# Attention with two mixture stages on one Trainium2 core: a hand order of three engines for the first eight head pairs

## The chip, the core and the metric

The kernel runs on one core of a Trainium2 chip. The core has TensorE (PE, with its weight loads as PEld), VectorE (DVE), ScalarE (ACT), GpSimd (POOL) and SyncE (SP), which only issues transfers here. GpSimd and ScalarE can issue transfers too. The metric is the device time of one launch in microseconds (us); lower is better.

## What is computed

Three stages follow each other: capped attention for 4 batches of 12 heads, 448 tokens, head size 64; a dense layer with a normalisation behind it; and a routed layer of eight experts, one for each token.

```python
scores = cap * tanh(q @ k.T / sqrt(D) / cap);  attn = exp(scores) / (sum + 1e-9);  x = attn @ v
h = x @ w_in;  solu = h * softmax(h);  ln = (solu - mean) / sqrt(var + 1e-6) * g_ln;  x = ln @ w_out
logits = x @ w_gate + modality_bias[modality_id];  e = argmax(logits);  gate = softmax(logits)[e]
out = gate * (relu(x @ w1[e]) @ w2[e])          # 1792 tokens, DM 768, DF 1024
```

## The kernel before

Heads are taken in 24 pairs, six to a batch. A pair is worked on in two units (cp 0 and 1), each with two of its four key chunks of 112. For pairs 0 to 7 ("plain") the scores are plain fp32 matmuls (a_scp, L664); from pair 8 on operands are split into high and low parts (a_split, a_sc). ScalarE does Tanh and Exp on each score tile (L667, L669). The value matmuls of a chunk (a_av, L714) come one unit behind its Exp. The sums over keys come straight from the exponentials by matmuls with a one-hot column for pairs below DIRECT = 6 (L720); from pair 6 on VectorE first adds the chunks (a_esp, L679 to L682) and one group of matmuls serves two pairs (L726). ScalarE or VectorE copies a pair's values to X (L729).

Meanwhile the weights w_in and w_out, which come as 64-bit words, are converted in 28 half blocks: GpSimd's queue loads one (conv_load, L450, four raw tiles), VectorE makes 32-bit numbers of it in three instructions (f64_to_f32, L426 to L428). For w_in (conv_in) ScalarE then casts a high part (L463) and VectorE subtracts (L464). For w_out (conv_out) VectorE scales by g_t and subtracts (L478, L479), TensorE transposes the block (conv_tr, L486), ScalarE copies the transposes (L488), and TensorE multiplies them by w_gate into eight more columns of w_out (conv_og, L494 to L496). Two blocks are converted in each unit (CUS), first the twelve of w_in, then the sixteen of w_out. The cast of a w_in block is put off to the next unit (defer(0)); conv_tr of the block before and conv_og stand right behind conv_out.

From unit 13 on batch 0 is finished: a_sums (L744), a_recip (L755 to L757), a_fin2 (L762 to L768). Then its token tiles are pushed: m_split, m_h (L536 to L538), m_act, m_tr (transposes L568, copies lh L576, ll L577) and m_y (L586 to L588) are a list of steps, which fill() deals out between the attention steps; pace() divides their cost by 27 + LEFT points, 33 for batch 1. Behind the attention come the routing and the expert slots: kinds D, H, F and T hold 512, 128, 256 and 32 tokens, in the order D, H, D, F, H, with T beside the first and third. Each block of expert weights is loaded by SP, cast by ScalarE (L1054) and subtracted by VectorE (L1055), some of them ahead of use; QH says how many steps before its end a slot H stops casting ahead.

What sets the order: inside manual_schedule the named engines keep the program's order. Before, that is TensorE alone up to the routing; ScalarE, VectorE, GpSimd and SP are ordered by the planner, by its own costs. PSUM has three slots of two banks for scores, transposes, logits, h and y (atile), one for values and one for sums. A tile's slot is freed when its last reader is done.

```python
with tc.manual_schedule(engines={mybir.EngineType.PE}):
    a_load(*pairs[0]); a_split(*pairs[0]); v_load(*pairs[0]); a_load(*pairs[1])
    ...
    setup_tables(xp)
    for n, (b, p) in enumerate(pairs):
```

Of the kernel before, what the change touches and what calls it, by code (L numbers as in the profile page):

```python
# [22 lines left out]
P = 128  # L23
# [36 lines left out]
TRP = (4, 0, 0)  # L60
TRO = 1
FIN = (2, 3, 4, 5, 5)
LEFT = (6, 6, 4)
RHA = 1
BIN = 0
SMD = (0, 1, 3, 4, 8, 12, 13)
# [16 lines left out]
def attn_moe_kernel(ctx, tc, qt, kt, vv, cap, w_in, w_out, g_ln, ids, w_gate, mbias, w1, w2, out):  # L83
# [49 lines left out]

    def setup_tables(tp):
        flat = tp.tile([P, NP, S], F32, tag="X", name="tmp").rearrange("p a b -> p (a b)")
# [12 lines left out]
        dve.tensor_add(sel, tmp, tmp2)  # L148
# [5 lines left out]
        pool.iota(pi, pattern=[[0, 1]], base=0, channel_multiplier=1, allow_small_or_imprecise_dtypes=True)  # L154
        pi2 = tm[:, 13:14]
# [5 lines left out]
        it = tm[:, 32:60].bitcast(I32).rearrange("p (t w) -> p t w", w=2)  # L161
        sp.dma_start(out=it, in_=ids)
        mb = tm[:, 64:80].rearrange("p (t w) -> p t w", w=NE)
        sp.dma_start(out=mb, in_=mbias)
# [12 lines left out]
        zr = flat[0:1, 2 * NP * P + 256:2 * NP * P + 256 + YW]  # L177
        dve.memset(zr, 0.0)
        sp.dma_start(out=ysc[0:1, :], in_=zr)

# [248 lines left out]

    later = {0: [], 1: [], 2: []}  # L430

    def defer(pos, f):
        if pos < 0:
            f()
        else:
            later[pos].append(f)

    def deferred(pos):
        while later[pos]:
            later[pos].pop(0)()  # L440

    blocks = [(w_in, 512, k, h) for k in range(ND) for h in range(2)] + \
        [(w_out, DM // 2, c, h) for c in range(NF) for h in range(2)]
    wraw = []

    def conv_load():
        if len(wraw) < len(blocks):
# [3 lines left out]
                         .bitcast(I32).rearrange("p (f t) -> p f t", t=2))  # L451
            wraw.append(raw)

    def conv_in(k, hf):
        raw = wraw[2 * k + hf]
        t = mp.tile([P, 512], I32, tag="x3", name=f"ti{k}_{hf}", bufs=4)
# [4 lines left out]

        def rest():
            act.copy(h_, tf)  # L463
            dve.tensor_sub(l_, tf, h_)  # L464

        defer(BIN, rest)

    wT = {}

    def conv_out(c, hf):  # L470
        HW_ = DM // 2
        raw = wraw[2 * ND + 2 * c + hf]
        t = mp.tile([P, HW_], I32, tag="x3", name=f"to{c}_{hf}", bufs=4)
# [5 lines left out]
        dve.scalar_tensor_tensor(l_, tf, g_t[:, c:c + 1], h_, op0=ALU.mult, op1=ALU.subtract)  # L479
        wT[c, hf] = tf  # L480

    def conv_tr(c, hf):
        tf = wT[c, hf]
        pt = atile(f"pt{c}_{hf}")[:, 0, :]
        for i in range(3):
            pe.transpose(pt[:, i * P:(i + 1) * P], tf[:, i * P:(i + 1) * P], ident)  # L486
        tt = mp.tile([P, 3, P], F32, tag="x3", name=f"wT{c}_{hf}", bufs=4)
        act.copy(tt, pt[:, :3 * P].rearrange("p (a b) -> p a b", a=3))  # L488
        wT[c, hf] = tt

    def conv_og(c):
        po = atile(f"po{c}")[:, 0, :]
        for i in range(ND):
            pe.matmul(po[:, :NE], wT[c, i // 3][:, i % 3, :], wg_t[:, i, :], start=(i == 0), stop=(i == ND - 1))  # L494
        act.activation(wouh[c][:, DM:YW], po[:, :NE], AF.Copy, scale=g_t[:, c:c + 1])
        dve.scalar_tensor_tensor(woul[c][:, DM:YW], po[:, :NE], g_t[:, c:c + 1], wouh[c][:, DM:YW],  # L496
                                 op0=ALU.mult, op1=ALU.subtract)

# [154 lines left out]
    def e_new(nm):  # L653
        return ap_.tile([CK, 2, S], F32, tag="e", name=nm, bufs=5)

    def a_scp(b, p, cp):

# [8 lines left out]
        for e, t in zip(es, ps):  # L666
            act.activation(e, t[:CK, :, :S], AF.Tanh, scale=sc8[:CK])  # L667
        for c, e in zip(chunks, es):
            act.activation(e, e, AF.Exp, scale=cap_t[:CK])  # L669
# [101 lines left out]

    crate = [0]
    convs = [(1, lambda k=k, h=h: conv_in(k, h)) for k in range(ND) for h in range(2)]
    for i in range(2 * NF + 2):
        if i < 2 * NF:
            convs.append((1, lambda c=i // 2, h=i % 2: conv_out(c, h)))
        if 0 < i <= 2 * NF:
            convs.append((0, lambda c=(i - 1) // 2, h=(i - 1) % 2: conv_tr(c, h)))
        if i > 1 and i % 2 == 1:
            convs.append((0, lambda c=(i - 3) // 2: conv_og(c)))  # L780

# [55 lines left out]

    with tc.manual_schedule(engines={mybir.EngineType.PE}):
# [6 lines left out]
        setup_tables(xp)  # L845
        for n, (b, p) in enumerate(pairs):
            for cp in range(2):
                if plain(b, p):
                    a_scp(b, p, cp)
                else:  # L850
                    a_sc(b, p, 0, cp)
                if cp == 0 and n:
                    a_av(*pairs[n - 1], chunks=(2, 3) if plain(*pairs[n - 1]) else range(4))
                elif cp and plain(b, p):
                    a_av(b, p, chunks=(0, 1))
                deferred(0)
                fill(FW[0])
                if b > 0:
                    finish(b - 1, 4 * p + 2 * cp)
                a_esp(b, p, cp)  # L860
                if cp == 0 and n + 1 < len(pairs):
                    a_split(*pairs[n + 1], js=(0,))
                if not plain(b, p):
                    a_sc(b, p, 1, cp)
                fill(FW[1])
                if cp == 1 and n + 1 < len(pairs):
                    a_split(*pairs[n + 1], js=(1,))
                if cp == 1 and n + 2 < len(pairs):
                    a_load(*pairs[n + 2])
                if cp == 0 and n + 1 < len(pairs):  # L870
                    v_load(*pairs[n + 1])
                fill(FW[2])
                while convs and (not convs[0][0] or CUS[crate[0]] <= 2 * n + cp):
                    crate[0] += convs[0][0]
                    convs.pop(0)[1]()
                if b > 0:
                    finish(b - 1, 4 * p + 2 * cp + 1)
        a_av(B - 1, NP - 1)
# [552 lines left out]
```

## Time and profile before

| | us |
|---|---|
| median of three runs | 782.14 (778.53 to 783.64) |
| the profiled execution | 780.17 |
| its span, first to last instruction | 778.4 |
| TensorE busy in the span | 733.1 (94%) |
| VectorE, ScalarE, GpSimd busy | 452.9, 392.1, 209.5 |

Times within the trace count from the span's start. A row of a timeline has start, duration, engine, line, operation, output and inputs, and a count when like instructions in a row are merged; in brackets stands how long the engine was idle before it and what released it. An fp32 matmul of the first eight pairs shows as two records, so x8 is four matmuls. In the table of stretches, PEclk is the granted TensorE clock: 1.00 is 2.4 GHz, 0.50 is 1.2 GHz, and means between them are a mixture of the two.

### The profile page before, as it was taken

Reading aid. Unit: us, or ns where it says so; the run is one execution under the profiler, and the core shown is the slowest. Engines: PE = TensorE matmul, PEld = TensorE weight load, DVE = VectorE, ACT = ScalarE, POOL = GpSimd, SP = SyncE. Lnnn points to the kernel's source line nnn. Section 1 sums busy time; section 2 is a strip of 40 time slices with the busy share of each in tenths; the row PEclk is TensorE's granted clock in tenths of the full one; section 3 lists DMA queues with packets and bytes.
Section 4 is the critical chain, followed back from the end, with each engine's and each line's share of the span. In section 5 each row is a group of like instructions: output and inputs, shape, how many; then the busy total and the mean of one; then the engine's idle time right before and its main releaser. Section 6 shows DMA issues by size and latency. Waiting matters only on the chain.

```text
span 778.4 us, 11381 instructions
## 1 busy us (share of the span) xinstructions
PE 733.1 (94%) x4150; PEld 575.0 (74%) x4150; DVE 452.9 (58%) x833; ACT 392.1 (50%) x541; POOL 209.5 (27%) x285
## 2 busy tenths in 40 slices
PE   6889889999999999999999999899999999999993
PEld 2235556777587787577878899789879988799982
DVE  5978766667757666674455744856146172563630
ACT  5987755776655464646641214434145171553530
POOL 4222013435352333345341214441210211002010
PEclk9999989999999999999999999999999999999996
DMA  9856302223312321322001303467937369485520
GB/s 290 295 175 170 100 14 71 83 84 91 94 53 75 91 75 43 103 54 74 22 0 42 123 21 123 143 236 253 385 106 250 132 202 395 162 262 172 205 79 23
DMA packets 39060, 104.50 MB, mean 134 GB/s; under 512 B 6439, under 2 KB 16689, under 8 KB 38994
## 3 DMA queue, kind: packets, MB, share of 16 engines
q1 hardware_dynamic: 32466, 74.26, 29.6%
q0 software_dynamic: 6528, 29.42, 10.9%
q8 instruction: 34, 0.56, 0.3%
q14 instruction: 32, 0.26, 0.1%
HBM read 92.58 MB, written 11.27 MB: 133 GB/s over the span
## 4 chain that ended last, share of the span: by engine, by line
PE 79%; DVE 7%; issue 6%; ACT 3%; DMA 3%; POOL 1%; SPq 0%; POOLq 0%; ACTq 0%; DVEq 0%
PE av L714 7%; PE h L536 5%; PE h L538 5%; PE h L537 5%; PE y L586 5%; PE y L588 5%; PE y L587 5%; PE sc L689 3%; PE sc L690 3%; PE poD L1178 3%; PE poD L1180 3%; PE poD L1179 3%; PE phD L1109 3%; PE phD L1110 3%; PE phD L1111 3%
## 5 line engine op out<-in xcount | busy, mean ns | idle before, releaser
L692 ACT ACTIVATE e<-sc,sc 112x896 f32<-112x896 f32 x64 | 64.5, 1008 | 76.6 <-PE sc L690 74.4
L714 PE MATMUL av<-e,v 112*64 112x448 f32 x384 | 81.3, 556 | 4.3 <-ACT e L669 2.4
L586 PE MATMUL y<-wouh,lh 128*128 128x388 f32 x224 | 77.1, 344 | 2.3 <-ACT lh L576 1.8
L588 PE MATMUL y<-wouh,ll 128*128 128x388 f32 x224 | 76.3, 341 | 0.3 <-DVE ll L577 0.2
L587 PE MATMUL y<-woul,lh 128*128 128x388 f32 x224 | 76.0, 339 | 0.0
L536 PE MATMUL h<-winh,xh 128*128 128x512 f32 x168 | 68.8, 410 | 1.5 <-ACT xh L523 1.5
L693 ACT ACTIVATE e<-e,cap_t 112x896 f32<-112x896 f32 x64 | 66.9, 1045 | 1.4
L538 PE MATMUL h<-winh,xl 128*128 128x512 f32 x168 | 66.7, 397 | 0.2 <-DVE xl L524 0.2
L537 PE MATMUL h<-winl,xh 128*128 128x512 f32 x168 | 66.3, 395 | 0.0
L714 PEld LDWEIGHTS av<-e,v 112*64 112x64 f32 x384 | 24.6, 138 | 52.8 <-issue 38.7
L701 POOL TENSOR_TENSOR es<-es,e 112x448 f32<-112x448 f32 x32 | 40.9, 1278 | 36.4 <-DVE es L700 33.0
L648 POOL TENSOR_TENSOR kl<-kr,kh 128x448 fp32r<-128x448 f32 x22 | 28.5, 1296 | 75.2 <-DVE kh L645 52.8
L586 PEld LDWEIGHTS y<-wouh,lh 128*128 128x128 f32 x224 | 42.1, 188 | 8.5 <-issue 4.3
L689 PE MATMUL sc<-qs,kh 128*112 128x448 f32 x128 | 47.3, 369 | 0.0
L690 PE MATMUL sc<-qs,kl 128*112 128x448 f32 x128 | 46.9, 366 | 0.0
L1055 DVE TENSOR_TENSOR wl_H<-raw_H,wh_H 128x768 fp32r<-128x768 f32 (+1 forms) x28 | 29.2, 1070 | 29.4 <-ACT wh_H L1054 29.4
L1055 DVE TENSOR_TENSOR wl_D<-raw_D,wh_D 128x768 fp32r<-128x768 f32 (+1 forms) x28 | 29.9, 1071 | 23.5 <-ACT wh_D L1054 23.2
L1178 PE MATMUL poD<-wh_D,hhD 128*128 128x384 f32 x128 | 43.0, 336 | 0.0
L588 PEld LDWEIGHTS y<-wouh,ll 128*128 128x128 f32 x224 | 42.1, 188 | 1.1 <-DVE ll L577 1.0
L1180 PE MATMUL poD<-wh_D,hlD 128*128 128x384 f32 x128 | 42.8, 334 | 0.0
L1179 PE MATMUL poD<-wl_D,hhD 128*128 128x384 f32 x128 | 42.8, 334 | 0.0
L587 PEld LDWEIGHTS y<-woul,lh 128*128 128x128 f32 x224 | 42.1, 188 | 0.8
(382 smaller groups left out, 1769.5 us busy)
## 6 DMA issues: line engine op xcount, KB each, us to landing
kr<-in_kt_dram SPq DMA_DIRECT2D x64, 112.0 KB, 2.6
qr<-in_qt_dram SPq DMA_DIRECT2D x64, 112.0 KB, 2.6
rawc<-in_w_in_dram POOLq DMA_DIRECT2D x12, 512.0 KB, 5.1
rawc<-in_w_out_dram POOLq DMA_DIRECT2D x16, 384.0 KB, 4.4
raw_D<-in_w_dram SPq DMA_DIRECT2D x12, 512.0 KB, 3.7
wr_T<-in_w_dram SPq DMA_DIRECT2D x16, 384.0 KB, 4.3
raw_D<-in_w_dram SPq DMA_DIRECT2D x16, 384.0 KB, 4.7
wr_T<-in_w_dram SPq DMA_DIRECT2D x12, 512.0 KB
```

What stands on the lines that cost most here:

```text
L536: pe.matmul(o, s["xh"][d], winh[d][:, c], start=(d == 0), stop=False)
L537: pe.matmul(o, s["xh"][d], winl[d][:, c], start=False, stop=False)
L538: pe.matmul(o, s["xl"][d], winh[d][:, c], start=False, stop=(d == ND - 1))
L586: pe.matmul(o, s["lh"][f], wouh[f][:, c], start=(f == 0), stop=False)
L587: pe.matmul(o, s["lh"][f], woul[f][:, c], start=False, stop=False)
L588: pe.matmul(o, s["ll"][f], wouh[f][:, c], start=False, stop=(f == NF - 1))
L689: pe.matmul(ps[:CK, c, :S], kh[:, k0:k0 + CK], qs, start=True, stop=False)
L690: pe.matmul(ps[:CK, c, :S], kl[:, k0:k0 + CK], qs, start=False, stop=True)
L693: act.activation(e, e, AF.Exp, scale=cap_t[:CK])
L714: pe.matmul(o[64 * j:64 * j + 64, :S], v[:, c, 64 * j:64 * j + 64], et[b, p, j, c], start=(c == 0), stop=(c == 3))
L1178: pe.matmul(p, hh[:, f, o], wh[:, c], start=(f == 0), stop=False)
L1179: pe.matmul(p, hh[:, f, o], wl[:, c], start=False, stop=False)
```

## The change

Pairs 0 to 7 (FIXED = 8) are put in a hand order for TensorE, ScalarE and VectorE together, in a new function unit(); pairs 8 to 23 go through the same function with TensorE alone ordered by hand. In a unit, conv_out no longer calls for its transposes at once: they go to a list "pe" that the next unit works off behind its scores, and conv_og to the list of the unit after that. The cast of a w_in block goes to a list "cast", worked off between the Tanh pair and the Exp pair, and the subtractions to "sub", worked off behind the conversions. The blocks of w_out and w_in alternate. The transposed block is kept in one tile of the tag ys instead of two of x3. setup_tables is split: the second half, which waits for the ids and biases, is at unit 3. g_t and wg_t are loaded by ScalarE's queue at the very start instead of SP's behind other loads. DIRECT becomes 8: pairs 6 and 7 are summed directly. For plain pairs finish() comes ahead of the values. QH's second number goes from 4 to 6, the second of LEFT from 6 to 7, and TRL = 3 puts the transposes of tile 9 (t = 9) three steps earlier in the list.

```diff
-DIRECT = 6
+DIRECT = 8
+FIXED = 8
-QH = (6, 4)
+QH = (6, 6)
+TRL = 3
-LEFT = (6, 6, 4)
+LEFT = (6, 7, 4)
...
+    def setup_second(tmp, tmp2, tm, ci, pi, it, mb):
+        dve.tensor_add(sel, tmp, tmp2)
...
-        sp.dma_start(out=g_t, in_=g_ln)
-        sp.dma_start(out=wg_t, in_=w_gate)
...
+    def flush(kind):
+        fs, later[kind] = later[kind], []
+        for f in fs:
+            f()
...
+    blocks = []
+    for i in range(2 * NF):
+        blocks.append((w_out, DM // 2, *divmod(i, 2)))
+        if i < 2 * ND:
+            blocks.append((w_in, 512, *divmod(i, 2)))
...
-        def rest():
+        def cast():
             act.copy(h_, tf)
-            dve.tensor_sub(l_, tf, h_)
+            later["sub"].append(lambda: dve.tensor_sub(l_, tf, h_))
-        defer(BIN, rest)
+        later["cast"].append(cast)
...
         wT[c, hf] = tf
+        later["pe"].append(lambda: conv_tr(c, hf))
...
+        act.copy(wT[c][:, 3 * hf:3 * hf + 3, :], pt[:, :3 * P].rearrange("p (a b) -> p a b", a=3))
+        if hf:
+            later["pe"].append(lambda: conv_og(c))
...
+    def unit(n, cp):
+        (b, p), u = pairs[n], 2 * n + cp
+        if plain(b, p):
+            a_scp(b, p, cp)
+            flush("pe")
+            flush("cast")
+            a_exp(b, p, cp)
+            if b > 0:
+                finish(b - 1, 4 * p + 2 * cp)
+        else:
+            a_sc(b, p, 0, cp)
+            flush("pe")
+            flush("cast")
+        if cp == 0 and n:
+            a_av(*pairs[n - 1], chunks=(2, 3) if plain(*pairs[n - 1]) else range(4))
+        elif cp and plain(b, p):
+            a_av(b, p, chunks=(0, 1))
+        fill(FW[0])
+        if b > 0 and not plain(b, p):
+            finish(b - 1, 4 * p + 2 * cp)
+        while convs and CUS[crate[0]] <= u:
+            crate[0] += 1
+            convs.pop(0)()
+        flush("sub")
+        if u == 3:
+            setup_second(*tables)
+        a_esp(b, p, cp)
...
+    with tc.manual_schedule(engines={ET.PE, ET.Activation, ET.DVE}):
+        act.dma_start(out=g_t, in_=g_ln)
+        act.dma_start(out=wg_t, in_=w_gate)
         a_load(*pairs[0])
-        a_split(*pairs[0])
         v_load(*pairs[0])
         a_load(*pairs[1])
         for _ in range(4):
             conv_load()
+        tables = setup_first(flat)
+        for n in range(FIXED):
+            unit(n, 0)
+            unit(n, 1)
+    with tc.manual_schedule(engines={ET.PE}):
+        for n in range(FIXED, len(pairs)):
+            unit(n, 0)
+            unit(n, 1)
...
-        msteps.insert(len(msteps) - TRO, (W[1], lambda: m_tr(t)))
+        msteps.insert(len(msteps) - TRO - TRL, (W[1], lambda: m_tr(t)))
```

## Rows read from the trace of the kernel before

**Rows 1.** Stretches: start:end, length, each engine's busy time, granted clock, DMA share, GB/s.

```profile
core 0: us, PE busy (x) PEld busy (x) DVE busy (x) ACT busy (x) POOL busy (x), PEclk, DMA share, GB/s
7.70:26.00 18.30, 16.92 (x82) 5.58 (x84) 13.74 (x32) 15.49 (x20) 3.09 (x6) 1.00 1.04 357
...
7.70:113.10 105.40, 92.90 (x506) 41.53 (x506) 80.24 (x174) 82.28 (x113) 17.20 (x28) 0.94 0.58 179
...
113.10:778.00 664.90, 640.22 (x3646) 533.43 (x3644) 369.71 (x651) 308.37 (x427) 185.74 (x243) 0.99 0.38 127
```

**Rows 2.** Two of the three stretches in which the granted clock is lower.

```profile
52.00:58.00 6.00, 6.00 (x27) 1.66 (x27) 3.06 (x7) 4.79 (x6) 0.98 (x2) 0.72 0.46 134
...
96.00:106.00 10.00, 8.22 (x35) 5.13 (x35) 3.48 (x9) 4.05 (x8) 0.00 (x0) 0.66 0.01 2
```

**Rows 3.** TensorE's waits, 7.7 to 114 us: total us, times, longest.

```profile
PE pt L486 <- DVE to L428: 4.1, 2, 2.0
PE av L714 <- ACT e L669: 2.4, 2, 1.4
PE po L494 <- ACT wT L488: 2.4, 3, 1.0
...
PE sc L664 <- DVE X L764: 1.6, 2, 1.2
```

**Rows 4.** Timeline of TensorE: one unit with two blocks, at full clock.

```profile
64.22 0.88 PE L486 MATMUL pt<-ident,to 128*128 128x128 f32 x6
64.93 1.42 PE L494 MATMUL po<-wg_t,wT 128*128 128x8 f32 x12
66.28 1.76 PE L664 MATMUL sc<-qr,kr 64*112 64x448 f32 x8
67.97 1.72 PE L714 MATMUL av<-e,v 112*64 112x448 f32 x8
69.63 0.96 PE L720 MATMUL S<-e,zone 112*32 112x448 f32 x8
70.52 0.87 PE L486 MATMUL pt<-ident,to 128*128 128x128 f32 x6
```

**Rows 5.** Timeline of TensorE: first scores, the end of batch 0, first h.

```profile
7.78 5.54 PE L664 MATMUL sc<-qr,kr 64*112 64x448 f32 x16 [7.78 <-DMA qr<-in_qt_dram]
...
100.87 0.92 PE L755 MATMUL rt<-ident,rr 112*44 112x112 f32 x4
...
106.45 1.49 PE L762 MATMUL rb<-rh,sel 128*128 128x448 f32 x6
...
113.16 0.50 PE L536 MATMUL h<-winh,xh 128*128 128x512 f32 x1
```

**Rows 6.** Timeline of ScalarE: two Tanh and two Exp.

```profile
13.88 1.89 ACT L667 ACTIVATE e<-sc,sc 112x896 f32<-112x896 f32 x2
15.66 1.97 ACT L669 ACTIVATE e<-e,cap_t 112x896 f32<-112x896 f32 x2
```

**Rows 7.** Stretch 7 to 113.1 us, instructions on es alone (PE, PEld, DVE, POOL).

```profile
7.00:113.10 106.10, 0.00 (x0) 0.00 (x0) 5.35 (x9) 0.00 (x0) 0.94 0.58 180
```

**Rows 8.** Timeline of VectorE: two independent neighbours, then two in a chain.

```profile
41.42 0.56 DVE L427 SCALAR_TENSOR_TENSOR to<-rawc,to 128x384 int32<-128x384 int32 x1
41.89 0.36 DVE L426 TENSOR_SCALAR to<-rawc 128x384 int32<-128x384 int32 x1
...
47.01 0.56 DVE L427 SCALAR_TENSOR_TENSOR to<-rawc,to 128x384 int32<-128x384 int32 x1
47.60 0.56 DVE L428 SCALAR_TENSOR_TENSOR to<-rawc,to 128x384 int32<-128x384 int32 x1
```

**Rows 9.** TensorE's waits, 630 to 645 us.

```profile
PE phD L1109 <- ACT txT L1206: 1.9, 1, 1.9
```

**Rows 10.** TensorE's waits, 404 to 414 us.

```profile
PE y L586 <- ACT lh L576: 0.9, 1, 0.9
```

**Rows 11.** DMA issues of the page: count, KB each, median us to landing.

```profile
rawc<-in_w_in_dram POOLq DMA_DIRECT2D x12, 512.0 KB, 5.1
```

More of the change, by code (lines that the diff above doesn't have):

```diff
@@ L154, in setup_tables @@
         pool.iota(pi, pattern=[[0, 1]], base=0, channel_multiplier=1, allow_small_or_imprecise_dtypes=True)
+        it = tm[:, 32:60].bitcast(I32).rearrange("p (t w) -> p t w", w=2)
+        sp.dma_start(out=it, in_=ids)
+        mb = tm[:, 64:80].rearrange("p (t w) -> p t w", w=NE)
+        sp.dma_start(out=mb, in_=mbias)
+        zr = flat[0:1, 2 * NP * P + 256:2 * NP * P + 256 + YW]
+        dve.memset(zr, 0.0)
+        sp.dma_start(out=ysc[0:1, :], in_=zr)
+        return tmp, tmp2, tm, ci, pi, it, mb
+    def setup_second(tmp, tmp2, tm, ci, pi, it, mb):
+        dve.tensor_add(sel, tmp, tmp2)
         pi2 = tm[:, 13:14]
@@ L428, in f64_to_f32 @@
         dve.scalar_tensor_tensor(dst, lo, 29, dst, op0=ALU.logical_shift_right, op1=ALU.bitwise_or)
-    later = {0: [], 1: [], 2: []}
-    def defer(pos, f):
-        if pos < 0:
-            f()
[L435 to L444, printed above, removed]
+    later = {"pe": [], "cast": [], "sub": []}
+    def flush(kind):
+        fs, later[kind] = later[kind], []
+        for f in fs:
+            f()
+    blocks = []
[3 more added lines that the diff above has]
+            blocks.append((w_in, 512, *divmod(i, 2)))
+    wraw, rawof = [], {}
     def conv_load():
@@ L452, in conv_load @@
             wraw.append(raw)
+            rawof[src is w_in, k, h] = raw
     def conv_in(k, hf):
-        raw = wraw[2 * k + hf]
+        raw = rawof[True, k, hf]
         t = mp.tile([P, 512], I32, tag="x3", name=f"ti{k}_{hf}", bufs=4)
@@ L471, in conv_out @@
         HW_ = DM // 2
-        raw = wraw[2 * ND + 2 * c + hf]
+        raw = rawof[False, c, hf]
         t = mp.tile([P, HW_], I32, tag="x3", name=f"to{c}_{hf}", bufs=4)
@@ L486, in conv_tr @@
             pe.transpose(pt[:, i * P:(i + 1) * P], tf[:, i * P:(i + 1) * P], ident)
-        tt = mp.tile([P, 3, P], F32, tag="x3", name=f"wT{c}_{hf}", bufs=4)
-        act.copy(tt, pt[:, :3 * P].rearrange("p (a b) -> p a b", a=3))
-        wT[c, hf] = tt
+        if hf == 0:
+            wT[c] = mp.tile([P, YW], F32, tag="ys", name=f"wT{c}", bufs=1)[:, :DM].rearrange("p (a b) -> p a b", b=P)
+        act.copy(wT[c][:, 3 * hf:3 * hf + 3, :], pt[:, :3 * P].rearrange("p (a b) -> p a b", a=3))
+        if hf:
+            later["pe"].append(lambda: conv_og(c))
     def conv_og(c):
@@ L493, in conv_og @@
         for i in range(ND):
-            pe.matmul(po[:, :NE], wT[c, i // 3][:, i % 3, :], wg_t[:, i, :], start=(i == 0), stop=(i == ND - 1))
+            pe.matmul(po[:, :NE], wT[c][:, i, :], wg_t[:, i, :], start=(i == 0), stop=(i == ND - 1))
         act.activation(wouh[c][:, DM:YW], po[:, :NE], AF.Copy, scale=g_t[:, c:c + 1])
-        dve.scalar_tensor_tensor(woul[c][:, DM:YW], po[:, :NE], g_t[:, c:c + 1], wouh[c][:, DM:YW],
-                                 op0=ALU.mult, op1=ALU.subtract)
+        later["sub"].append(lambda: dve.scalar_tensor_tensor(
+            woul[c][:, DM:YW], po[:, :NE], g_t[:, c:c + 1], wouh[c][:, DM:YW], op0=ALU.mult, op1=ALU.subtract))
     rpool = []
@@ L667, in a_scp, with a_exp @@
             act.activation(e, t[:CK, :, :S], AF.Tanh, scale=sc8[:CK])
-        for c, e in zip(chunks, es):
+        exps[b, p, cp] = es
+    def a_exp(b, p, cp):
+        for c, e in zip((2 * cp, 2 * cp + 1), exps.pop((b, p, cp))):
             act.activation(e, e, AF.Exp, scale=cap_t[:CK])
@@ L772, in attn_moe_kernel @@
     crate = [0]
[L773 to L780, printed above, removed]
+    convs = [lambda f=conv_in if src is w_in else conv_out, k=k, h=h: f(k, h) for src, _, k, h in blocks]
     msteps, drained = [], set()
@@ L836, in finish @@
             pace(3 * (2 * NP - (FIN[4] + 1) // 2) + LEFT[b])
-    with tc.manual_schedule(engines={mybir.EngineType.PE}):
+    def unit(n, cp):
[25 more added lines that the diff above has]
+        a_esp(b, p, cp)
+        if cp == 0 and n + 1 < len(pairs):
+            a_split(*pairs[n + 1], js=(0,))
+        if not plain(b, p):
+            a_sc(b, p, 1, cp)
+        fill(FW[1])
+        if cp == 1 and n + 1 < len(pairs):
+            a_split(*pairs[n + 1], js=(1,))
+        if cp == 1 and n + 2 < len(pairs):
+            a_load(*pairs[n + 2])
+        if cp == 0 and n + 1 < len(pairs):
+            v_load(*pairs[n + 1])
+        fill(FW[2])
+        if b > 0:
+            finish(b - 1, 4 * p + 2 * cp + 1)
+    ET = mybir.EngineType
+    flat = xp.tile([P, NP, S], F32, tag="X", name="tmp").rearrange("p a b -> p (a b)")
+    with tc.manual_schedule(engines={ET.PE, ET.Activation, ET.DVE}):
+        act.dma_start(out=g_t, in_=g_ln)
+        act.dma_start(out=wg_t, in_=w_gate)
         a_load(*pairs[0])
-        a_split(*pairs[0])
         v_load(*pairs[0])
@@ L844, in attn_moe_kernel @@
             conv_load()
[L845 to L877, printed above, removed]
+        tables = setup_first(flat)
[6 more added lines that the diff above has]
+            unit(n, 1)
         a_av(B - 1, NP - 1)
```

13 lines of the change are left out of this document (2 added, 11 removed).

## The prediction

> **What bounds the kernel now.** The first view is the table of stretches, which splits the span where the first h matmul starts [rows 1]. Behind it TensorE is busy 640.2 of 664.9 us, and the next engine, VectorE, 370: that stage is TensorE's own work, and nothing that this change does to its work list matters there. Ahead of it, from the first score matmul at 7.78 to the first h matmul at 113.16 [rows 5], TensorE is busy 92.9 of 105.4 us and its clock averages 0.94, while VectorE (80.2) and ScalarE (82.3) are loaded but not full [rows 1]. So the first sixteen units (a unit is half a pair: four of its eight score matmuls) run at (113.2 - 7.8) / 16 = 6.6 us each, and some of that is waiting. The second view says what for: the 12.5 us of idle time are transposes waiting for a w_out block that VectorE has only just made (4.1), the logit matmuls waiting for ScalarE's copy of those transposes (2.4), the value matmuls waiting for Exp (2.4), scores waiting for X (1.6), and smaller ones [rows 3]. Both of the first two come from the code: conv_tr and conv_og stand directly behind conv_out in TensorE's hand order. The third view shows a second price: the granted clock falls to the 1.2 GHz level in three stretches, each some microseconds behind such a wait; two of them are shown, 6 us at a mean of 0.72 (the third is like it) and 10 us at 0.66, so 1.7 + 1.7 + 3.4 = 6.8 us are lost to half speed [rows 2].
>
> **The change, part by part.** *The order of the first eight pairs.* Transposes of a block now come one unit after its conversion, its logit matmuls one unit later still, behind the scores, and the cast of a w_in block between the Tanh pair and the Exp pair. What TensorE then has to do up to the first h is a sum of groups at full clock, start to start [rows 4]: 16 units of scores at 1.69 = 27.0; 15 of values at 1.66 = 24.9; 16 transposes of half a block at 0.71 / 2 = 5.7; 8 logit groups at 1.35 = 10.8; sums by direct matmul in 15 units at 0.89 = 13.4; the reciprocal and fin2 steps 0.9 + 1.5 [rows 5] and as much as the reciprocal again for a_sums (an estimate, 0.9). Together 85.1, from 7.8: 92.9 us. The direct sums of pairs 6 and 7 are in it with 3 x 0.89 = 2.7 that were not there before; the fourth group falls behind the first h, where one group of the old sums goes.
>
> To that come waits that I expect to stay. In the first units nothing hides Exp: by the sum of its groups TensorE could start unit 4 at about 24.7, while ScalarE, at 1.78 for two Tanh start to start and 1.97 for two Exp [rows 6], with the first copies and casts between, lets it at about 26.3: 1.6. Around fin2 the scores wait for X as now, 1.6 [rows 3], the reciprocal of batch 0 stands on VectorE behind the last two conversions, about 0.5, and the split behind the last Exp, about 0.6: 2.7 (the last two estimates). A logit tile keeps one of three PSUM slots until VectorE's subtraction, which now stands behind that unit's two conversions and, from unit 3 on, behind setup_second too. If the next scores take another slot, that costs nothing; if the planner gives them this one, up to 2.6, half of VectorE's 5.0 us a unit (worked out below), which is the most that I see it trail there. I take 1.3. Small waits that I cannot place: between 0 and the 12.5 of now; I take 2, nearer to 0 because the two largest causes are named and moved. The clock: between 0 and the 6.8 of now; I take 0, because each of the three falls follows waits of 0.6 to 2.0 us on the moved steps, and the stretch to 26 us, with 1.4 us of idle time in it, shows 1.00 [rows 1]. First h at 92.9 + 1.6 + 2.7 + 1.3 + 2 = 100.5 against 113.2: 12.7 us saved.
>
> *The other engines have to hold that pace.* ScalarE's work there does not change: 82.3 of what becomes 92.7 us, 89%. VectorE loses nine adds, 5.35, from this stretch [rows 7], but a block's conversion is now issued as an unbroken chain. Instructions that depend on each other start 0.59 apart where the same kind behind an independent one needs 0.47 [rows 8]: 0.12 a link, four links in each of 16 w_out blocks and two in each of 12 w_in blocks, 10.6 us if none was chained before, 0 if all were. Some of those chains were unbroken already (the second pair of [rows 8] is one), so I take half: 80.2 - 5.4 + 5.3 = 80.1 of 92.7, 86%, or 5.0 a unit. Covered, but the cover is thin, and that is a rival below.
>
> The Trainium skill (VectorE: DVE Perf Modes, The DRAIN you can't avoid) says that the next operation cannot issue before the pipe is empty, whether or not operations are chained by semaphores. By it the chain would cost nothing and VectorE would come to 74.9; the 0.59 against 0.47 of [rows 8] disagree, and the rows decide.
>
> *g_t and wg_t by ScalarE's queue.* w_out blocks come first now, so VectorE needs g_t for its very first block instead of behind twelve others. It is moved ahead of SP's q, k and v loads and past the small tables on that queue; two issues on ScalarE, which has no work before the first scores, cost nothing. Had it stayed on SP, it would have held VectorE until those loads were done. Splitting the setup takes the wait for the ids away from VectorE's head; at unit 3 it costs the VectorE time counted above. The transposed copy in the ys tile instead of x3 is one tile per block; its next writer stands behind the logit matmuls of the block before on TensorE, so no new wait.
>
> *Later edits.* TRL puts the transposes of tile 9 three steps, some 1.6 us, ahead: the 0.9 wait for lh goes [rows 10]. QH lets slot H cast fewer blocks ahead: before, ScalarE's copy txT stood behind casts that waited for their DMA, and TensorE waited 1.9 for it [rows 9]; now one such cast is ahead of it, which has its data. The casts that follow are due only a block (about 5.6 us) later. Gain 1.9, or 0 if the next cast is late instead. LEFT spreads the same steps over 34 instead of 33 points: nothing, since TensorE is full there.
>
> Sum: 12.7 + 0.9 + 1.9 = 15.5. The profiled execution took 780.2, so 764.7; its time is 2 us below the median of 782.1, which the new runs should be held to: 766.6, say 766.5.
>
> **The rivals.** *A, the waits go altogether* (no slot wait, nothing unplaced): 3.3 less, 763; the far end of it is an earlier unit 4. *B, VectorE becomes the bound.* Each unit ends on VectorE with subtractions that wait for ScalarE's casts, which stand behind the copy of a transpose; if about 1 us of that waiting is not covered, VectorE's unit is 5.0 + 1 = 6.0 and 14 units lose 0.7 each against TensorE's mean 5.3: 10 us back, 776. For it: 86% load. Against: the conversions of the next unit need nothing from this one but a tile two units old. *C, the gain is partly given back behind the stage*, where ScalarE, VectorE and GpSimd are still ordered by the planner, and their order is formed anew: TensorE's idle time there, 24.7 us with the end of the program [rows 1], has some 12 of waits within; half as much again makes 772.5. For it: every engine's order there may change. Against: they are about half idle.
>
> *D, slower: a weight block lands late.* All three orders now hang on one transfer. Four raw tiles, two used in a unit: a load has two units less one conversion, 2 x 5.3 - 2.4 = 8.2 us. Landing takes 5.1 [rows 11]; beyond 8.2 the unit is (L + 2.4) / 2, and at L = 10.8 it is the 6.6 of now, from where on the change loses. At 12 the fourteen units with blocks take 7.2: first h at 100.5 + 14 x 1.9 = 127, so 780.2 + 14 - 2.8 = 791, 793 by the median. For it: in the first 18 us the transfers fill all engines (share 1.04) [rows 1]. Against: they then move 357 GB/s, and a unit needs 0.92 MB of blocks (512 and 384 KB) and 0.34 of q, k and v in 5.3 us, 238. The Trainium skill (Perfetto Trace Analysis, Tensor Engine Instruction) has the other engines' queues as strict FIFO, which is what would hand one late block to everything behind it; whether that happens no row of before shows.
>
> **How the numbers follow.** Forecast 0.53 (its own range 760 to 771), A beyond it 0.07, B 0.17, C 0.10, D 0.13 (from hardly any gain to 793). A measurement of this kernel tells about 1%, 774 to 790, from no change. Faster: forecast, A, half of B and most of C, 0.53 + 0.07 + 0.08 + 0.06 = 0.74; same: the rest of B and C and a third of D, 0.09 + 0.04 + 0.04 = 0.17; slower 0.09. The range goes from 757 (A with an earlier start) to 780, B and C in it: what is left out is about D and a little below.
>
> **What would show it.** First h at about 100 (below 104); the waits for pt and po near zero there; a granted clock of 1.00 from 26 to 100; the two later waits gone. A first h above 106 with TensorE waiting for transposes, casts or VectorE's PSUM slot says B; VectorE waiting for rawc says D; a first h near 100 with a time above 771 says C. A clock still at 1.2 GHz somewhere says that the waits were not its cause.

## The result, and the profile after

The changed kernel takes 769.42 us (median of 4 runs, 768.61 to 771.15) against 781.08 (778.53 to 783.64) for the kernel before in the same comparison: a ratio of 0.9854, 95% interval 0.9815 to 0.9893, 11.7 us less. A second measurement beside the last experiments gave 768.98 against 781.16: 0.9829, interval 0.9797 to 0.9860. Forecast were 766.5 (757 to 780) and "faster", so direction, size and mechanism came about; some 3.5 of the 15.5 us of the sum did not come, and several of its terms were sized wrongly in ways that mostly cancelled.

The profiled execution of the changed kernel is its longest run, 771.15 with a span of 769.5 (the other runs' spans lie between 766.9 and 767.7). Its table of stretches answers to [rows 1]: start:end, length, each engine's busy time, granted clock, DMA share, GB/s; the split is again at the first h matmul.

```profile
core 0: us, PE busy (x) PEld busy (x) DVE busy (x) ACT busy (x) POOL busy (x), PEclk, DMA share, GB/s
7.60:102.30 94.70, 92.18 (x530) 39.56 (x530) 77.47 (x160) 79.43 (x112) 14.82 (x27) 0.96 0.61 194
102.30:769.00 666.70, 642.59 (x3647) 536.29 (x3644) 371.59 (x652) 310.12 (x429) 186.32 (x244) 0.99 0.38 127
```

The first stage is 10.7 us shorter (105.4 before), and TensorE idles in it 2.5 us instead of 12.5. VectorE is 82% busy and ScalarE 84%, so neither became the bound. Of the 10.7 us, 10.0 are idle time and 3.4 time at the lower clock (6.8 before, 3.4 now, below); the 2.7 of the direct sums go off. But the clock still averages 0.96 there, and the second stage is 1.8 us longer than the 664.9 of before, not 2.8 shorter.

TensorE's waits in the first stage, up to 110 us (total us, times, longest), answer to [rows 3]; the first line is the start of the program:

```profile
PE sc L670 <- DMA qr<-in_qt_dram: 7.6, 1, 7.6
PE sc L670 <- ACT e L673: 1.1, 1, 1.1
PE pt L488 <- ACT e L673: 0.9, 2, 0.7
PE po L498 <- DVE woul L500: 0.3, 1, 0.3
PE po L498 <- DVE X L773: 0.2, 1, 0.2
```

The transposes' wait for VectorE (4.1), the logit matmuls' wait for wT (2.4) and the value matmuls' wait for Exp (2.4) are gone. What is left is five short waits, the two longest (1.1 of the scores, 0.7 of the transposes) for a PSUM slot that Tanh (L673) still reads.

TensorE's timeline shows the new unit, first with and then without logits, and the first h:

```profile
33.69 1.76 PE L670 MATMUL sc<-qr,kr 64*112 64x448 f32 x8
35.38 1.50 PE L498 MATMUL po<-wg_t,wT 128*128 128x8 f32 x12
...
39.74 1.76 PE L670 MATMUL sc<-qr,kr 64*112 64x448 f32 x8
41.43 0.55 PE L488 MATMUL pt<-ident,to 128*128 128x128 f32 x3
41.91 1.72 PE L723 MATMUL av<-e,v 112*64 112x448 f32 x8
43.56 0.96 PE L729 MATMUL S<-e,zone 112*32 112x448 f32 x8
...
102.39 0.50 PE L540 MATMUL h<-winh,xh 128*128 128x512 f32 x1
```

No bracket stands in the unit: every group follows the one before it. A unit without logits takes 4.71 us (39.74 to 44.45), one with logits 6.05 (33.69 to 39.74), a mean of 5.38; the forecast's groups made 5.27 (1.69 + 1.66 + 0.71 / 2 + 1.35 / 2 + 0.89), before it was 6.6.

TensorE's waits behind the first stage, 110 to 770 us, the longest two and those of the later edits:

```profile
PE y L590 <- DVE lg L594: 1.8, 1, 1.8
PE h L540 <- ACT xh L527: 1.5, 1, 1.5
...
PE y L590 <- ACT lh L580: 1.0, 1, 1.0
```

The wait for txT [rows 9] is gone and one of the two waits for lh too [rows 10], as forecast. The first line is new: before, y waited for lg 0.4 us.

Finally the stretches of the changed kernel where the clock falls:

```profile
24.00:30.00 6.00, 5.66 (x25) 1.91 (x27) 5.70 (x18) 4.11 (x7) 1.07 (x2) 0.72 0.97 316
...
88.00:94.00 6.00, 5.74 (x30) 3.60 (x28) 2.17 (x5) 4.55 (x8) 0.00 (x0) 0.72 0.01 3
290.00:302.00 12.00, 9.91 (x49) 9.00 (x48) 10.26 (x19) 4.92 (x6) 6.40 (x9) 0.86 0.23 64
310.00:320.00 10.00, 8.16 (x27) 5.77 (x27) 8.22 (x15) 5.87 (x8) 3.56 (x3) 0.83 0.27 86
```

Each is a time at the 1.2 GHz level that costs 1.7 us ((1 - 0.72) x 6; (1 - 0.86) x 12; (1 - 0.83) x 10): 3.4 us in the first stage, where the forecast had 0 and the kernel before 6.8 [rows 2], and 3.4 in the second, where the kernel before has none. (In every execution the clock falls once more behind TensorE's last matmul, which ends some 14 us before the span does; that fall delays no matmul and is left out here.)

### The profile page after: what moved, and what is told of

Its sections match the earlier page's. It is cut to its first block, busy times and chain, and to the rows that moved or that the text cites. A ratio compares the mean times of both kernels' runs of the same rounds, so it can differ in the third digit from the quotient of the medians.

```text
span 769.5 us, 11411 instructions
## 1 busy us (share of the span) xinstructions
PE 734.8 (95%) x4174; PEld 575.9 (75%) x4174; DVE 452.3 (59%) x821; ACT 391.0 (51%) x541; POOL 207.6 (27%) x285
## 4 chain that ended last, share of the span: by engine, by line
PE 86%; DVE 5%; ACT 3%; issue 3%; DMA 1%; SPq 0%; POOL 0%; POOLq 0%; DVEq 0%; ACTq 0%
PE av L723 9%; PE h L540 5%; PE h L542 5%; PE h L541 5%; PE y L590 5%; PE y L591 5%; PE y L592 5%; PE sc L698 3%; PE sc L699 3%; PE poD L1200 3%; PE poD L1202 3%; PE poD L1201 3%; PE phD L1132 3%; PE phD L1133 3%; PE phD L1131 3%
## 5 line engine op out<-in xcount | busy, mean ns | idle before, releaser
L540 PEld LDWEIGHTS h<-winh,xh 128*128 128x128 f32 x168 | 31.8, 189 | 15.2 <-issue 6.5
```

The source lines that it names most:

```text
L540: pe.matmul(o, s["xh"][d], winh[d][:, c], start=(d == 0), stop=False)
```

## The experiments

Theory when they began: the edits add up; the first stage gives nearly what was forecast, through the order of the transposes; the rest is lost to the new wait for lg, which LEFT = 7 makes, and to the clock. Rivals: the parts help each other, so that none gives its share alone; or the planner's new order behind the stage eats the gain (the forecast's rival C). The runs came in three sets, each beside its own runs of the kernel before: 781.9, 781.63 and 781.16 us.

**The stage alone, and the later edits alone.** The first kernel keeps the new first eight pairs and takes back the rest:

```diff
-QH = (6, 6)
+QH = (6, 4)
-TRL = 3
+TRL = 0
-LEFT = (6, 7, 4)
+LEFT = (6, 6, 4)
```

> The changed kernel with its three late edits undone (QH, LEFT and TRL as before), so the hand order, the queue of the norm weights and the direct sums alone. Theory S, the gain is the first stage's: first h at 102.4 as in the changed kernel, the wait for txT (1.9) and one for lh (0.9) are back, the time is 1.5 to 3 us above the changed kernel's 769.4: 771 to 772.5. Rival T, the late edits carry the gain: time above 776.

Measured: 770.0 (769.64 to 770.35), ratio 0.9858, interval 0.9829 to 0.9887: 11.9 us, first h at 102.2. The second kernel is the reverse: the kernel before, with QH = (6, 6), LEFT = (6, 7, 4) and the transposes of tile 9 three steps ahead.

> The kernel before with the three late edits alone (QH, LEFT, TRL). Theory S: first h stays at 113, the two late waits (1.9 and 0.9) go, time 2 to 3 us below before: 778 to 779.5. Rival T: below 774. Rival N, other casts become late: within 1 us of before.

Measured: 780.72 (778.66 to 784.13, 10 runs), ratio 0.9989, interval 0.9964 to 1.0014. So the stage is the whole gain, and the later edits together give 1.2 us, within the spread, instead of 2.8. Neither time came out as expected: the first kernel is 0.6 us above the changed one, not 1.5 to 3, and the second lies between what theory S and rival N expected. The next runs show why. In the first kernel TensorE's waits from 630 us on show the price that QH takes away:

```profile
PE phD L1131 <- ACT txT L1228: 2.7, 1, 2.7
```

That is 2.7 us here, not the 1.9 of [rows 9].

**LEFT.** One number back, `LEFT = (6, 7, 4)` to `(6, 6, 4)`, all else as changed:

> The changed kernel with LEFT's second number back at 6. In the changed kernel TensorE waits 1.84 for a y slot at 295.7 and its clock is at 0.83 to 0.93 from 290 to 320, which the kernel before does not show. Theory L, the slower pace of batch 1 moved that y group against VectorE's lg: the wait falls below 0.6 and the clock there is 1.00; time 3 to 5 us lower, 764 to 767. Rival P, the planner's order of VectorE is formed anew whatever the pace: wait and clock stay, time within 1.5 us of 769.4.

Measured: 767.18 (766.3 to 769.52), ratio 0.9831, interval 0.9798 to 0.9863; first h at 99.83. The other half of theory L, a clock of 1.00 there, did not come: left6 loses 3.4 us to the clock behind the stage, as the changed kernel does (table further below). To settle whether the 2.2 us are real, both kernels ran once more side by side:

> The changed kernel once more, beside the one that differs only in LEFT. If the 1.8 us wait of y for lg and the lower clock behind it come from LEFT = 7: y waits for lg 1.8 us again, 769.4 (768.5 to 771). First h between 99.5 and 102.5, by where the clock falls in the first stage in this execution; if the falls at 24 and 88 us belong to the instruction stream, 102.2 to 102.5 again.

> The changed kernel with LEFT = (6, 6, 4), once more. LEFT = 7 costs 2.2 us: 767.2 (766.5 to 768.5), 2 us under the changed kernel of the same call, y waiting for lg 0.4. The rival, that LEFT costs nothing as the prediction had it and the 2.2 were the spread of runs: within 0.8 us of the changed kernel. First h 99.8 if the clock's falls belonged to the stream, 99.5 to 102.5 if they vary from execution to execution.

Measured: 768.98 (767.64 to 770.61) and 766.51 (765.59 to 767.83), 6 runs each, 2.5 us apart. LEFT = 7 costs 2.2 to 2.5 us. How it does is seen in two timelines of the changed kernel's repeat, VectorE's and then TensorE's:

```profile
295.06 1.43 DVE L557 TENSOR_SCALAR u<-u,sm 128x1024 f32<-128x1024 f32 x1
296.41 0.17 DVE L758 COPY rr<-rr 112x48 f32<-112x48 f32 x1
296.50 0.61 DVE L709 TENSOR_TENSOR es<-es,e 112x448 f32<-112x448 f32 x1
297.04 0.21 DVE L594 SCALAR_TENSOR_TENSOR lg<-y,sm,bias_t 128x8 f32<-128x8 f32 x1
```

```profile
295.13 0.33 PE L592 MATMUL y<-wouh,ll 128*128 128x388 f32 x1
297.31 0.44 PE L590 MATMUL y<-wouh,lh 128*128 128x388 f32 x1 [1.85 <-DVE lg L594]
```

y ends at 295.46 and its PSUM tile is wanted again at once, but lg, which reads the logits out of it, stands on VectorE behind the normalisation of u (1.43), a copy and an add. With one step of batch 1 moved, the end of a y tile falls into that queue. With LEFT = 6 the same wait is 0.43 us, on TensorE's timeline of left6_again:

```profile
292.65 0.45 PE L590 MATMUL y<-wouh,lh 128*128 128x388 f32 x1 [0.43 <-DVE lg L594]
```

It is 1.8 or 1.9 in all seven profiles with LEFT = 7 and 0.4 in all seven with LEFT = 6, that of the kernel before among them. This wait is 1.4 of the 2.2 to 2.5 us; TensorE's idle time behind the first h is 1.7 to 1.9 us less with LEFT = 6 (table further below), and what the rest is made of is not shown.

**The two later edits, taken apart.** LEFT = 6 and, in addition, `TRL = 0`, so that only QH is left:

> The changed kernel with LEFT = (6, 6, 4) and TRL = 0: only QH is left of the later edits. The prediction has 0.9 us for TRL: 768.1, with y waiting for lh twice (1.8) instead of once (1.0). If TRL gives nothing because the step that is moved only changes places: 767.2 and the waits as long in sum.

Measured: 766.36 (765.22 to 768.97, 6 runs), against 766.51 with TRL = 3: nothing in the time. TensorE's waits behind the stage, with TRL = 0 first, then with TRL = 3:

```profile
PE y L590 <- ACT lh L580: 1.8, 2, 1.0
...
PE r_sm L391 <- DVE r_more L382: 1.2, 1, 1.2
```

```profile
PE phD L1131 <- DVE e_ob L999: 1.3, 1, 1.3
...
PE y L590 <- ACT lh L580: 1.0, 1, 1.0
```

The 0.9 of [rows 10] goes as forecast. Beside it the wait of r_sm for r_more (1.2) gives way to one of phD for e_ob (1.3), but that is not TRL's: og6 and tail6, both with TRL = 3, show both of these waits. TensorE's idle time behind the first h is 0.8 to 0.9 us less with TRL = 3. What hides it in the time may be the clock: the profiled executions with TRL = 3 lost 3.4 us in the second stage, the one with TRL = 0 none (table further below), and over six runs each the granted clock averaged 0.9873 with TRL = 3 and 0.9893 with TRL = 0. Whether these falls come with the moved step is not shown. The two edits without LEFT on the kernel before:

> The kernel before with QH (6, 6) and the transposes of the last tile three steps ahead, LEFT left at (6, 6, 4). If the two later edits are worth 2.8 us on their own and LEFT = 7 took it back in the earlier run of all three (-1.2): 779.0 against 781.8, y waiting for lg 0.4, no wait for txT. If the two are worth only the 1.2 that all three gave: 780.6.

Measured: 780.26 (775.37 to 783.78, 12 runs), ratio 0.9985, interval 0.9958 to 1.0011. The median is nearer to the second expectation, but that does not tell the two apart: the kernel before spreads over 8 us by itself. Behind the faster stage, stage_only to left6 in one set gave 2.8.

**What in the stage does it: the place of the transposes.** The new hand order stays, but each block's transposes, and the logits right behind them, are issued behind the unit's conversions. That is closer than before, where the transposes were those of the block before and the logits stood one more step behind:

```diff
             convs.pop(0)()
+        while later["pe"]:
+            flush("pe")
         flush("sub")
```

> The changed kernel, but each unit works off its transposes and logits right behind its conversions, as before the change; all else, the hand order of the three engines too, stays. Theory W, it is the delay that removes TensorE's waits: waits for a converted block and for the transposed copy come back in most units, first h at 112 or later (102.4 in the changed kernel), time 779 or more. Rival H, the order of ScalarE and VectorE alone is enough: first h below 106, time below 774.

Measured: 785.56 (782.1 to 787.32, 10 runs), ratio 1.0052, interval 1.0027 to 1.0077; first h at 114.7. All of the gain is gone, and the old waits are back, that of the logits longer than before (2.4) and that of the transposes shorter (4.1), TensorE's from 5 to 115 us:

```profile
PE po L498 <- ACT wT L491: 4.5, 6, 1.3
PE pt L488 <- DVE to L429: 2.8, 3, 2.0
```

So the distances from conversion to transposes and from there to logits are a necessary part: without them the rest of the change gains nothing. That it comes out slower than before may be the closer logits, and how much each of the two distances is worth was not tried. Of the 12.3 us by which the first h is later, 5.1 are time at the lower clock (8.5 instead of 3.4, table further below). No run has the delay without the rest of the new stage, or the new stage with the old order of the blocks (w_in first), so what those are worth stays open.

**ScalarE's and VectorE's order.** The first eight pairs are written out by hand for TensorE alone, and the planner orders the other two:

```diff
-    with tc.manual_schedule(engines={ET.PE, ET.Activation, ET.DVE}):
+    with tc.manual_schedule(engines={ET.PE}):
```

> The changed kernel with TensorE alone ordered by hand for the first eight pairs; ScalarE and VectorE are left to the planner as before. Theory P, the delay of transposes and logits on TensorE is what removes the waits: first h between 101 and 105, time 768 to 772. Rival H, the order of ScalarE and VectorE matters by itself (casts and chains taken out of turn as before): first h above 106, time above 773.

Measured: 773.4 (772.52 to 774.66), ratio 0.9896, interval 0.9867 to 0.9926; first h at 107.0. TensorE waits for ScalarE again, 5 to 108 us:

```profile
PE pt L488 <- ACT e L673: 2.7, 4, 0.8
PE sc L670 <- ACT e L673: 2.3, 2, 1.2
PE pt L488 <- ACT e L678: 1.1, 1, 1.1
```

Against the changed kernel that is 4.0 us by the times, 3.3 by the ratios, out of 11.7. Both numbers came out as rival H had them, so the order of ScalarE and VectorE matters by itself; the gain that is left without it, 7.7 to 8.4 us, is the larger part. The first h is 4.6 us later, 1.7 of it at the lower clock.

**g_t and wg_t.** Back on SP's queue, behind the loads and tables ahead of them:

```diff
-        act.dma_start(out=g_t, in_=g_ln)
-        act.dma_start(out=wg_t, in_=w_gate)
...
         tables = setup_first(flat)
+        sp.dma_start(out=g_t, in_=g_ln)
+        sp.dma_start(out=wg_t, in_=w_gate)
```

> The changed kernel with g_t and wg_t loaded by SP behind q, k, v and the tables, as before. By the prediction g_t then lands behind SP's loads, as the ids did (14.2 in the kernel before), and VectorE, which needs it at 8.9, waits 4 to 6 us; the first transpose, now at 12.6, comes 3 to 6 us later and first h 2 to 5 us later. Rival: VectorE's lag is made good by unit 4, first h within 1 us.

Measured: 774.25 (773.02 to 778.57, 7 runs), ratio 0.9905, interval 0.9867 to 0.9944; first h at 107.2. VectorE's longest wait in the first stage, and then TensorE's longest behind the start:

```profile
DVE wouh L479 <- DMA g_t<-in_g_ln_dram: 4.8, 1, 4.8
```

```profile
PE pt L488 <- DVE woul L500: 3.4, 2, 2.2
```

The norm weights (4 KB) are issued at 5.28 us instead of 0.80, and VectorE's first product waits for them until 13.66 instead of starting at 8.90; 4.8 us later first h is 4.8 us later too. The first transposes are not late (11.96 us, 12.55 in the changed kernel; they do not need g_t), which the expectation had wrong; TensorE first feels the delay in its waits of the next units. One late small load was handed on through all three hand-written orders, in full as far as can be told: without the clock's loss the first h of one order varies by 1.4 us (table further below), so that the two numbers agree to the tenth is luck. The Trainium skill (Perfetto Trace Analysis, Tensor Engine Instruction) has VectorE's queue as strict FIFO; the trace agrees, since the next block's conversion, at 10.11 in the changed kernel, starts only at 14.66, behind the products, and waits for nothing else.

**The direct sums of pairs 6 and 7.** `DIRECT = 8` back to `6`, so that VectorE adds es for these two pairs as before:

> The changed kernel with DIRECT back at 6: pairs 6 and 7 are summed by VectorE's adds and one matmul group. By the sum, TensorE loses 2.7 us of work ahead of the first h and VectorE gets back 5.3 us. Theory P, TensorE bounds the stage: first h 1.5 to 2.7 us earlier or the same time, no new waits. Rival V, VectorE is the bound by units 12 to 15, where its conversions stand ahead of the reciprocal of batch 0: first h 2 to 5 us later.

Measured: 770.7 (769.53 to 773.43), ratio 0.9855, interval 0.9803 to 0.9907; first h at 104.15. On VectorE's timeline the adds stand ahead of batch 0's rh, which moves from 88.27 to 90.51:

```profile
87.94 0.62 DVE L690 TENSOR_TENSOR es<-es,e 112x448 f32<-112x448 f32 x1
...
90.51 0.62 DVE L766 TENSOR_TENSOR rh<-rt,rh 12x448 fp32r<-12x448 f32 x1
```

First h is 1.8 us later, but 1.7 of that is a longer time at the lower clock in this one execution. Without the clock's loss it is where it was, although TensorE has 2.7 us less to do. That work turned into waits, which theory P did not expect; TensorE's, 5 to 105 us, beside the one for the slot of Tanh:

```profile
PE po L498 <- DVE woul L500: 1.1, 1, 1.1
PE h L540 <- ACT xh L527: 1.0, 1, 1.0
```

In the whole time 770.7 cannot be told from 769.0 to 769.4 across sets. What the direct sums are worth stays open, between 0 and 1.7 us.

**The wait at unit 14.** VectorE's logit subtraction is put ahead of the unit's conversions, with LEFT = 6, so that the PSUM slot comes free earlier:

```diff
+        flush("og")
         while convs and CUS[crate[0]] <= u:
```

> The changed kernel with LEFT's second number at 6, and VectorE's subtraction of the logit columns ahead of the unit's conversions instead of behind them, so that the logit tile gives its PSUM slot back earlier. Theory S, that slot is what holds the scores of unit 14 (1.1 us) and the transposes of unit 3: these waits go and first h comes 1 to 2 us earlier than the same kernel without it (99.8), time 765 to 767. Rival V, VectorE now waits for the logit matmuls at the head of each odd unit and trails: new waits for conversions, first h later than 101, time 769 or more.

Measured: 768.63 (768.2 to 768.82), ratio 0.9834, interval 0.9783 to 0.9886; first h at 101.8. The 1.1 us wait is gone: there the second half of the scores had waited for the slot of the first, while the logits held another until VectorE's subtraction (88.02 in the changed kernel). But VectorE now waits for ScalarE at the head of its queue:

```profile
DVE woul L500 <- ACT wouh L499: 4.9, 3, 3.2
```

No gain over left6. The slot term of the forecast is real (1.1), and this way around it gains nothing in the whole time.

**The clock, over all profiled executions.** From the granted clock in windows of 2 us, (1 - clock) x 2, summed up to the first h and behind it; the last column is TensorE's idle time from the first h to its last matmul:

```
kernel        first h  lost in stage  first h less loss   rest of span  lost there  rest less loss   idle there
before         113.16       6.8           106.3              665.2         0.0          665.2         11.5
after          102.39       3.4            99.0              667.1         3.4          663.7         10.6
after_again    102.11       3.4            98.7              665.3         1.7          663.6         10.5
left6           99.83       0.0            99.8              664.7         3.4          661.2          8.7
left6_again    101.08       1.7            99.4              664.9         3.4          661.5          8.8
og6            101.75       1.7           100.0              664.8         1.7          663.0         10.1
trl0           101.86       3.4            98.4              663.0         0.0          663.0          9.6
stage_only     102.20       3.4            98.8              665.6         0.0          665.6         11.8
direct6        104.15       5.1            99.0              667.6         3.4          664.2         10.9
gt_sp          107.18       3.4           103.8              665.3         1.7          663.6         10.5
planner_ad     107.03       5.1           101.9              665.9         1.7          664.2         10.9
tr_now         114.73       8.5           106.2              665.7         0.0          665.7         12.0
tail_only      116.84      10.2           106.6              665.6         1.7          663.9         10.7
tail6          113.05       8.5           104.5              663.2         0.0          663.2          9.9
```

Six of these executions issue the same work in the first stage in the same order (after, left6, their repeats, trl0, stage_only). Without the loss their first h lies between 98.4 and 99.8; with it, between 99.8 and 102.4. So the loss is not fixed by the order: it is 0, 1.7 or 3.4 us from one execution to the next. But the three executions with the old order (before, tail_only, tail6) and tr_now, where TensorE waits most, lost 6.8 to 10.2. In the last but one column og6 differs from left6 by 1.5 to 1.8 us with the same later edits, 1.3 to 1.4 of it idle time, so remainders there tell an edit's worth only to about 2 us.

## Why the prediction was right, and where its sum was off

**The stage: forecast 12.7 us, measured 11.9** (stage_only). The mechanism is the one named: the transposes no longer wait for VectorE, nor the logits for ScalarE, and putting them back takes all of the gain (tr_now). The sum had 92.7 us from the first scores to the first h, 7.8 to 100.5; left6, in the one execution that lost nothing to the clock, shows 7.08 to 99.83: 92.75. That it fits so well is luck: the groups came to 90.3 instead of 85.1, and the waits (1.6 + 6.0 in the sum) to 2.4, so errors of 5.2 in either direction cancelled.

- *The groups* were 2.9 + 1.8 us too short, and smaller pieces more. I counted the first two units' scores at 1.69 each, but the first sixteen matmuls take 4.9 to 6.3 us (6.25 in left6, against 3.38), which the 5.54 of [rows 5] had shown. And I halved the transposes of a block, 0.71 / 2 = 0.36, where three alone take 0.48 start to start: a part of the group does not shrink with its number. Twelve of the sixteen stand alone, 12 x 0.12 = 1.4, and the last four, in two units, took 0.35 more. One term was too long: the reciprocal's 0.9 was read where the clock was low ([rows 5] at 100.87, [rows 2]); at full clock it is 0.49.
- *The start* (1.6, unit 4 held by Exp): in left6 unit 4 starts at 27.11 and TensorE does not wait at all before it; the delay of unit 4, forecast at 26.3, is that of the first scores. As a wait it is 0, wrong in its cause.
- *The other waits* (2.7 + 1.3 + 2 = 6.0): 2.4 us in left6, the slot wait of 1.1 the largest, and 0.4 for X.
- *The clock* (0): 0 to 3.4, and 3.4 in the profiled execution, so the granted clock of 1.00 from 26 to 100 that the forecast named as its sign did not come. "Each of the three falls follows waits of 0.6 to 2.0 us on the moved steps" took their cause from where they stood. The trace of before had the counterexample: a 2.05 us wait on the same steps, the longest of the stage, with the clock at 1.00 for 8 us behind it (timeline, then table of stretches). The bounds 0 to 6.8 held the loss; a value in between would have been the better choice.

```profile
44.07 0.52 PE L486 MATMUL pt<-ident,to 128*128 128x128 f32 x3 [2.05 <-DVE to L428]
```

```profile
44.00:52.00 8.00, 7.01 (x45) 3.67 (x45) 6.84 (x15) 7.53 (x11) 1.94 (x4) 1.00 0.64 194
```

**VectorE and ScalarE hold the pace**, as forecast: 82% and 84% instead of 86% and 89%, and no wait for them but the slots; rival B did not come about. The conversions are chains now, with the 0.59 of [rows 8] in every one, VectorE's timeline of the changed kernel:

```profile
12.29 0.56 DVE L428 SCALAR_TENSOR_TENSOR to<-rawc,to 128x384 int32<-128x384 int32 x1
12.88 0.57 DVE L429 SCALAR_TENSOR_TENSOR to<-rawc,to 128x384 int32<-128x384 int32 x1
```

VectorE's total fell from 80.2 to 77.5, the adds took 5.35 away, so what came in is 2.6, half of the 5.3 that I allowed. The busy time leaves out the short gaps in a chain, though (0.03 us between the two rows above), and holds other work: the conversions alone, each instruction from its start to the next start less waits, grew from 66.3 to 70.5 us, 4.2 of the 5.3. The choice of half was nearly right. (The section of the Trainium skill from which the prediction worked out 74.9, VectorE: DVE Perf Modes, The DRAIN you can't avoid, also says that a next operation which is not held starts earlier; so 0.47 beside 0.59 does not contradict it, and the 74.9 does not follow from it.) planner_ad shows that the hand order is what keeps the load harmless: with the planner the first h is 4.6 us later, 2.9 to 3.2 without the clock's loss.

**g_t on ScalarE's queue costs nothing**: right, VectorE's first product at 8.90 without a wait; and what it avoids, that VectorE would be held, is 4.8 us (gt_sp). Blocks landed in time, so rival D did not come about.

**QH: forecast 1.9.** Right in mechanism; 2.8 by the times with TRL in it (stage_only to left6, one set), 3.6 for QH alone (stage_only to trl0, across sets), 2.7 by the wait that it takes away, 2.2 by TensorE's idle time. **TRL: forecast 0.9, measured 0 in the time, 0.8 to 0.9 in TensorE's idle time**: the wait goes as forecast, and a larger loss to the clock, for which the sum had no term there, may hide what it is worth.

**LEFT: forecast nothing, measured +2.2 and +2.5 us.** This is the step that failed. "Nothing, since TensorE is full there" looked at TensorE's work alone. A step that moves on a full engine still moves the moment at which it needs a PSUM tile back, and that tile is freed by VectorE's lg, in VectorE's order: a small form of the forecast's rival C, in one place and with one cause.

Together: -11.9 (stage) - 2.8 (QH and TRL) + 2.3 (LEFT) = -12.4, against -11.7 and -12.2 measured. These are steps along one row of kernels, from stage_only by left6 to the changed one, so they have to come near the whole and do not show that the edits add up. On the kernel before QH and TRL take 1.6 us of TensorE's idle time away (11.5 to 9.9, tail6), behind the new stage 3.0 to 3.1 (11.8 to 8.7 and 8.8), so they are not worth the same everywhere. The changed kernel with LEFT = (6, 6, 4) is faster than the changed kernel and stage_only, 767.18 and 766.51 us in two sets (0.9831, interval 0.9798 to 0.9863; 0.9797, interval 0.9767 to 0.9827).

## What to carry to other kernels

Where one engine makes what another consumes, put the consumer a unit of work later in the bounding engine's order rather than making the producer faster: without that nothing of the gain was left here, and a hand order on the helpers and an early issue of a 4 KB load were needed to keep it whole (3 to 4 and 4 to 5 us). When a step is moved on an engine that is full, look at who must free the buffer that it writes and what stands ahead of that instruction on its own engine. Count groups from rows of the same size as those that will run, not from halves of larger ones.

## What the runs showed of the hardware that was not expected

The granted clock falls to the 1.2 GHz level behind waits of about a microsecond, but the same wait in the same place is followed by a fall in one execution and not in another. TensorE waits 1.11 us at unit 14 in every execution of this order. TensorE's timeline of the changed kernel's repeat, and its table of stretches from 80 to 94 us:

```profile
78.45 0.55 PE L488 MATMUL pt<-ident,to 128*128 128x128 f32 x3 [0.15 <-ACT e L673]
...
86.66 1.01 PE L670 MATMUL sc<-qr,kr 64*112 64x448 f32 x4 [1.11 <-ACT e L673]
```

```profile
80.00:94.00 14.00, 12.60 (x60) 4.67 (x62) 7.83 (x18) 7.84 (x12) 1.13 (x1) 0.76 0.02 6
```

The same two views of left6:

```profile
85.16 1.01 PE L670 MATMUL sc<-qr,kr 64*112 64x448 f32 x4 [1.11 <-ACT e L673]
```

```profile
80.00:94.00 14.00, 12.36 (x73) 5.37 (x72) 10.47 (x21) 7.98 (x12) 1.15 (x1) 1.00 0.09 25
```

The first of these executions was at the lower level twice there, once before that wait (from 80 to 84), with nothing but the 0.15 us of the first line near ahead of it:

```profile
82.00:84.00 2.00, 2.00 (x10) 0.20 (x8) 1.90 (x5) 0.00 (x0) 0.00 (x0) 0.51 0.00 0
```

Behind the 1.50 us wait of h for xh left6 shows 0.86 from 300 to 312 us, trl0 1.00 from 302 to 314:

```profile
300.00:312.00 12.00, 10.48 (x40) 6.62 (x37) 8.56 (x16) 6.18 (x9) 4.30 (x4) 0.86 0.28 92
```

```profile
302.00:314.00 12.00, 10.33 (x46) 6.45 (x41) 9.60 (x17) 7.22 (x10) 4.34 (x4) 1.00 0.27 91
```

So most falls stand behind a wait, but whether one comes differs from execution to execution; what decides it was not tried. The Trainium skill (TensorE: Matmul & The Clock Gate, What's actually happening) says that the window in which activity is judged runs free of the kernel, and that one kernel therefore shows different counts of slow matmuls from run to run; it says so of the warm-up at the start. The differences from one execution to the next in these rows (0.76 against 1.00 from 80 to 94 us) fit with that in the middle of a kernel too; no run here shows the window itself.
